# Gate weights loaded in an earlier stage, a place of its own for one raw tile, and other slots for two weight units in a fused mLSTM and mixture kernel

## The chip, the cores and the metric

The kernel runs on one core of one Trainium2 chip. The metric is the device time of the program in microseconds (us), median of several executions of the same program on the same inputs. Less is better.

## The reference

Three stages follow one another, all in fp32:

```python
x = mlstm(q, k, v, i_gate, f_gate, o_gate)        # (2, 8, 768, 40) -> x: 1536 tokens x 320
h = x @ w_in                                      # 320 x 2048
x = np.maximum(0.01 * h, h) @ w_out               # 2048 x 320
logits = x @ w_gate                               # 320 x 8
P = np.exp(logits - logits.max())
for _ in range(8):
    P /= P.sum(1, keepdims=True) + 1e-09
    P /= P.sum(0, keepdims=True) + 1e-09
    P *= 1536 / 8
out = sum(P[:, e:e+1] * (np.maximum(x @ w1[e], 0) @ w2[e]) for e in range(8))   # w1: 320 x 1024, w2: 1024 x 320
```

The last stage is dense: every token goes through all 8 experts, weighted by its column of P.

## The kernel before, in words

Precision first. Every product of two fp32 matrices is made of fp32r pieces: a factor is split into a high part (an ACT copy, `high7` L207 or L198) and a low part (the factor minus its high part, `low7` L210, `rest7` L214, L199, on DVE or POOL), and the product is the sum of three or four matmuls.

**First part** (up to the line `ctx.enter_context(tc.manual_schedule())`, L720). The attention runs in chunks of 128 tokens beside the first feed-forward, which goes through 96 steps of `up` (L520) and `down` (L532). Functions hang on these steps by number (`step(g, fn)`); in this part the framework may still reorder the instructions of each engine. The weights `w_in` and `w_out` come through three slots of the pool tag `raw`, loaded from the SP queue. Near the end of this part the first third of what the next stage needs is made: the tiles of x for the first half of the tokens (q = 0, class `Position`, x0), and the weights of expert units 0, 1 and 2.

**Second part.** From that line on the order written in the code is the order on each engine. The 8 experts make 32 units (`experts`, class `Products`, 256 hidden columns each; e0_3 is unit 3, e1_0 unit 4). The tokens are in two halves q, so there are 64 passes, in the order `order` (L818): units 0, 1, 2 with q = 0, then with q = 1, then unit 3 with both, unit 4 with both, and so on. The hidden layer of a pass, `up_c(i)` (L837), is a two by two block product done with seven block products instead of eight: seven calls of `product` (four matmuls each, L830 to L833) on sums and differences of blocks of the weights and of x. Four PSUM banks hold the results; ACT, DVE and POOL form from them the hidden tiles `hh` (high) and `hl` (low). `down_c(i)` (L880) multiplies these with `w2` for six token tiles (L157 to L159), in three PSUM banks by turns, and adds each result to `acc` (DVE L899 to L903, and ACT L897 for every second tile of unit 0).

The loop at the end emits `up_c(i+1)` and then `down_c(i)`. I call that **step i+1**: step 0 is `up_c(0)` alone, step 6 is `up_c(6)` with `down_c(5)`. Extra work hangs in by `when(g, slot, fn)` or `hook(g, slot, fn)`: slots 0 to 6 of g lie in `up_c(g+1)`, one behind each of its seven products, slots 7 to 12 in `down_c(g)`, one behind each tile. So (g, slot) always lies in step g+1. In this stretch hang:

- the x tiles of the second half of the tokens (x1). For each third p of them: `repeat` (POOL copies), `turn` (four transposes on TensorE into the one bank of `ps_s`, and an ACT copy into the raw tile, twice), `sums` (four subtractions, DVE), and the split into X[1] (`high` on ACT, `low` on DVE, `rest` on POOL). X[1] is first read by pass 3.
- the gate: the weights `wg` (loaded and split at L733 to L740), four `logits` in step 2, `logits_turn` and the maximum in step 3, and the eight rounds of row and column division in steps 4 to 7, two in each: `columns` on TensorE at slots 2 and 8, then `columns_end` and `rows` at slots 4 and 10, eight short DVE operations (L803 to L806, L793 to L796) that the next `columns` needs.
- the weights of units 3 and on: `load1` (ten DMAs into a `raw` slot), `sums` (four POOL operations, L186), `split1` in two halves (ACT copy L207, POOL L210 and L214), `load2`, `split2` (ACT L198, POOL L199).

The pool tag `raw` has three slots for all raw tiles of this stretch; a new tile takes over the slot of an earlier one and waits until that one's last use is over. Three lines show how the extra work is hung in:

```python
        when(g, s, x1[p].turn, k, ps_s)                    # L927
    for n in range(3, NU):
        u, g = experts[n], max(2 * n - 4, 3)               # L953: unit 3 has g = 3, unit 4 has g = 4
        hook(g - 2, 0, u.load1)
```

Of the kernel before, what the change touches and what calls it, by code (L numbers as in the profile page):

```python
# [37 lines left out]
def mlstm_moe_kernel(ctx, tc, qp, q3, kp, kn, vn, gates_in, og, cst_in, scr_in, w_in, w_out, w_gate, w1, w2, out):  # L38
# [35 lines left out]
    rc = cst[0:R, P + GV + 8:P + GV + 14]  # L74

# [140 lines left out]
    class Position:  # L216
# [62 lines left out]
    with ExitStack() as st1:  # L279
# [451 lines left out]

    wgr = cp.tile([P, 4, E], F32, tag="wgr", name="wgr")
    nc.gpsimd.memset(wgr, 0.0)  # L733
    for h in range(2):
        nc.sync.dma_start(wgr[:, 2 * h], w_gate[:, h])
        for r in (0, 2):
            nc.sync.dma_start(wgr[r * KM:(r + 1) * KM, 2 * h + 1], w_gate[h * KM:(h + 1) * KM, 2])
    wg = cp.tile([P, 4, 2, E], F32R, tag="wg", name="wg")
    nc.vector.tensor_copy(wg[:, :, 0, :], wgr)
    nc.vector.tensor_tensor(wg[:, :, 1, :], wgr, wg[:, :, 0, :].bitcast(F32), op=ALU.subtract)  # L740

    lT = cp.tile([2 * E, NT], F32, tag="lT", name="lT")
# [3 lines left out]
    K3 = 3 * KM  # L746

    def logits(q, i):
# [201 lines left out]
    when(-1, 3, experts[1].split2, GP)  # L950
    when(0, 12, experts[2].split2, GP)
    for n in range(3, NU):
        u, g = experts[n], max(2 * n - 4, 3)  # L953
        hook(g - 2, 0, u.load1)
        for k in range(4):
            hook(g, 8 + k, lambda u=u, k=k: u.sums(nc.gpsimd, (k,)))
        hook(g + 1, 8, lambda u=u: u.split1(0, nc.gpsimd, nc.gpsimd))
        hook(g + 1, 10, lambda u=u: u.split1(1, nc.gpsimd, nc.gpsimd))
        hook(g + 1, 12, u.load2)
        hook(g + 2, 8, lambda u=u: u.split2(nc.gpsimd))  # L960
# [117 lines left out]
```

## Time and profile before

| | before |
|---|---|
| median of 3 runs | 997.86 us (993.4 to 997.95) |
| the profiled execution: time, span | 997.24 us, 995.4 us |
| TensorE (PE) busy | 957.5 us, 96% of the span |
| VectorE (DVE), ScalarE (ACT), GpSimd (POOL) busy | 598.0, 485.7, 613.0 us |
| mean granted TensorE clock | 0.966 |

The span is the time from the first to the last instruction of the profiled execution. PE is the matrix engine, PEld its weight loads. The granted clock is a share of 2.4 GHz; TensorE has two levels, 1.0 (2.4 GHz) and 0.5 (1.2 GHz), so a stretch with 0.81 spent 0.38 of its time at 1.2 GHz. In rows of the timeline a value in brackets is the engine's idle time before the instruction and what ended it.

### The profile page before, as it was taken

The numbers are of one execution on the slowest core, as the hardware profiler recorded it, in microseconds if no ns is written. First come the engines' busy times: TensorE is split into PE (matmuls) and PEld (weight loads), VectorE is DVE, ScalarE is ACT, GpSimd is POOL, SyncE is SP. The second block draws the span as 40 slices with busy tenths as digits, with TensorE's granted clock in tenths as the row PEclk, the third lists the DMA queues.
The fourth block names the chain that finished last, engine by engine and source line by source line (L and its number), as shares of the span: only waits on it lengthen the run. The fifth ranks groups of instructions, "written<-read, shape, count | busy, mean of one in ns | idle before, by whom it ended". The sixth has DMA issues, their size and how long they took to land.

```text
span 995.4 us, 16898 instructions
## 1 busy us (share of the span) xinstructions
PE 957.5 (96%) x6188; PEld 924.0 (93%) x6188; DVE 598.0 (60%) x1159; ACT 485.7 (49%) x953; POOL 613.0 (62%) x616
## 2 busy tenths in 40 slices
PE   8699899999998997999999999999999999999998
PEld 4599898999997787899999999999999999999998
DVE  6989524142464566756656666666656566665655
ACT  4646344534655433564545454454545454454542
POOL 4553643443474434677777767677777767777762
PEclk9579999999997998999999999999999999999999
DMA  8544212011110200111111111111111111111102
GB/s 274 195 152 134 86 54 75 29 52 38 27 57 1 64 2 14 48 36 42 49 49 36 35 52 45 43 36 41 51 48 36 36 47 47 46 36 36 47 1 80
DMA packets 57160, 56.63 MB, mean 57 GB/s; under 512 B 7558, under 2 KB 47670, under 8 KB 57078
## 3 DMA queue, kind: packets, MB, share of 16 engines
q1 hardware_dynamic: 57078, 55.56, 18.6%
q8 instruction: 48, 0.79, 0.3%
q14 instruction: 34, 0.28, 0.1%
HBM read 53.57 MB, written 1.97 MB: 56 GB/s over the span
## 4 chain that ended last, share of the span: by engine, by line
PE 79%; DVE 9%; ACT 3%; POOL 3%; issue 2%; DMA 2%; SPq 1%; DVEq 0%; ACTq 0%; POOLq 0%
PE y L157 11%; PE y L158 11%; PE y L159 11%; PE b L833 8%; PE b L830 7%; PE b L832 7%; PE b L831 7%; PE ha L150 6%; PE ya L157 2%; PE ya L159 2%; PE ya L158 2%; PE yps L456 2%; PE sps L442 1%; PE zps L460 1%; DMA raw_a<-in_w_out_dram 1%
## 5 line engine op out<-in xcount | busy, mean ns | idle before, releaser
L852 POOL TENSOR_TENSOR hl<-c,hh 128x384 fp32r<-128x384 f32 x192 | 196.6, 1024 | 201.1 <-ACT c L851 176.5
L157 PE MATMUL y<-w_e,hh 128*128 128x320 f32 x768 | 238.7, 311 | 1.8 <-ACT acc L897 0.9
L158 PE MATMUL y<-w_e,hh 128*128 128x320 f32 x768 | 237.3, 309 | 0.0
L159 PE MATMUL y<-w_e,hl 128*128 128x320 f32 x768 | 236.8, 308 | 0.0
L903 DVE SCALAR_TENSOR_TENSOR acc<-y,Pg,acc 128x320 f32<-128x320 f32 x336 | 179.3, 548 | 63.7 <-PE y L159 56.1
L850 ACT ACTIVATE hh<-c 128x384 fp32r<-128x384 f32 x192 | 99.7, 519 | 226.9 <-DVE c L849 226.9
L830 PE MATMUL b<-X,w_e 128*128 128x384 f32 x448 | 154.5, 345 | 2.5 <-DVE s L861 2.0
L832 PE MATMUL b<-X,w_e 128*128 128x384 f32 x448 | 153.6, 343 | 2.2 <-POOL w_e L210 2.2
L833 PE MATMUL b<-X,w_e 96*128 96x384 f32 x448 | 154.1, 344 | 1.3 <-POOL w_e L214 1.3
L831 PE MATMUL b<-X,w_e 128*128 128x384 f32 x448 | 152.5, 340 | 0.0
L157 PEld LDWEIGHTS y<-w_e,hh 128*128 128x128 f32 x768 | 144.3, 188 | 3.9 <-DVE acc L899 1.5
L158 PEld LDWEIGHTS y<-w_e,hh 128*128 128x128 f32 x768 | 144.3, 188 | 0.0
L159 PEld LDWEIGHTS y<-w_e,hl 128*128 128x128 f32 x768 | 144.1, 188 | 0.0
L529 POOL TENSOR_TENSOR hla<-gg,hha 128x256 fp32r<-128x256 f32 x90 | 76.7, 856 | 85.5 <-ACT hha L528 72.5
L150 PE MATMUL ha<-xT,w_a 128*128 128x256 f32 x768 | 115.1, 293 | 6.8 <-DVE xT L269 3.5
L150 PEld LDWEIGHTS ha<-xT,w_a 128*128 128x128 f32 x768 | 105.1, 198 | 11.8 <-DVE xT L269 4.0
L851 ACT ACTIVATE c<-c 128x384 f32<-128x384 f32 x192 | 100.8, 525 | 17.4
L849 DVE TENSOR_TENSOR c<-b,s 128x384 f32<-128x384 f32 x192 | 100.5, 551 | 13.1 <-PE b L833 8.0
L868 DVE SCALAR_TENSOR_TENSOR hl<-b,hh 128x384 fp32r<-128x384 f32 x64 | 35.7, 558 | 103.1 <-ACT hh L867 103.1
L830 PEld LDWEIGHTS b<-X,w_e 128*128 128x128 f32 x448 | 86.0, 192 | 3.9 <-DVE s L861 2.9
L832 PEld LDWEIGHTS b<-X,w_e 128*128 128x128 f32 x448 | 85.6, 191 | 2.8 <-POOL w_e L210 2.8
L833 PEld LDWEIGHTS b<-X,w_e 96*128 96x128 f32 x448 | 85.8, 191 | 1.9 <-POOL w_e L214 1.9
(159 smaller groups left out, 1555.7 us busy)
## 6 DMA issues: line engine op xcount, KB each, us to landing
raw_e<-in_w_dram SPq DMA_DIRECT2D x32, 320.0 KB, 2.9
raw_e<-in_w_dram SPq DMA_DIRECT2D x62, 128.0 KB, 2.2
raw_e<-in_w_dram SPq DMA_DIRECT2D x248, 32.0 KB, 1.8
raw_a<-in_w_in_dram SPq DMA_DIRECT2D x8, 768.0 KB, 5.0
raw_a<-in_w_out_dram SPq DMA_DIRECT2D x8, 640.0 KB, 4.4
R<-in_kp_dram SPq DMA_DIRECT2D x11, 256.0 KB, 2.7
R<-in_qp_dram SPq DMA_DIRECT2D x11, 256.0 KB, 3.6
R<-in_vn_dram SPq DMA_DIRECT2D x11, 184.5 KB, 2.5
```

The lines of the kernel that those rows point to most:

```text
L150: nc.tensor.matmul(h_ps, t1[:, ws, c * P:(c + 1) * P], xt[:, xs, t0:t0 + n], start=(j == 0), stop=(j == len(MM1) - 1),)
L157: nc.tensor.matmul(y_ps, a, t2[:, c, :], start=first, stop=False)
L158: nc.tensor.matmul(y_ps, a, t2[:, 2 + c, :], start=False, stop=False)
L159: nc.tensor.matmul(y_ps, b, t2[:, c, :], start=False, stop=last)
L830: nc.tensor.matmul(bank, f[:, 0], b[:, 0], start=fresh, stop=False, skip_group_check=not fresh)
L831: nc.tensor.matmul(bank, f[:, 0], b[:, 2], start=False, stop=False, skip_group_check=not fresh)
L832: nc.tensor.matmul(bank, f[:, 2], b[:, 0], start=False, stop=False, skip_group_check=not fresh)
L833: nc.tensor.matmul(bank, f[0:K3, 1], b[0:K3, 1], start=False, stop=True, skip_group_check=not fresh)
L849: nc.vector.tensor_tensor(c, part, plus, op=ALU.add)
L851: nc.scalar.activation(c, c, AF.Relu)
L852: nc.gpsimd.tensor_tensor(hl[a][b], c, hh[a][b].bitcast(F32), op=ALU.subtract)
L903: nc.vector.scalar_tensor_tensor(out=o, in0=y, scalar=Pg[:, 2 * HP * q + t, e:e + 1], in1=o, op0=ALU.mult, op1=ALU.add)
```

## The change

1. The gate weights `wg` and their raw tile `wgr` move to a pool that lives through the whole kernel. Their six DMAs (`load_gate`, hung at step 64 of the first feed-forward) and their two DVE operations (`split_gate`, at step 70) are now in the first part. The clearing of `wgr` goes from POOL to DVE.
2. The raw tile of x for p = 1 (second half of the tokens) is a tile `rawE` of its own. The tile `lT` of the transposed logits, which had a place of its own, becomes a `raw` slot.
3. The x1 work hangs at other slots: the third p = 1 two slots earlier and its split later, the third p = 2 two slots earlier. `split2` of unit 1 moves from (-1, 3) to (-1, 6).
4. Unit 3: `sums` from (3, 8 to 11) to (2, 0 to 3), `split1` from (4, 8) and (4, 10) to (3, 0) and (3, 7), `load2` from (4, 12) to (3, 9), `split2` from (5, 8) to (4, 0). Unit 4: `load1` from (2, 0) to (2, 5), `sums` from (4, 8 to 11) to (4, 1 to 4), `split1` from (5, 8) and (5, 10) to (5, 0) and (5, 7), `load2` from (5, 12) to (5, 9), `split2` from (6, 8) to (6, 0). Units 5 and on stay.

```diff
+    wg = const.tile([P, 4, 2, E], F32R, tag="wg", name="wg")
+    wgr = const.tile([P, 4, E], F32, tag="wgr", name="wgr")
+    def load_gate():
+        nc.vector.memset(wgr, 0.0)
+        for h in range(2):
+            nc.sync.dma_start(wgr[:, 2 * h], w_gate[:, h])
+            for r in (0, 2):
+                nc.sync.dma_start(wgr[r * KM:(r + 1) * KM, 2 * h + 1], w_gate[h * KM:(h + 1) * KM, 2])
+    def split_gate():
+        nc.vector.tensor_copy(wg[:, :, 0, :], wgr)
+        nc.vector.tensor_tensor(wg[:, :, 1, :], wgr, wg[:, :, 0, :].bitcast(F32), op=ALU.subtract)
...
-        def turn(self, k, pool):
+        def turn(self, k, pool, home=None):
...
-                self.raw = wp.tile([P, 7, 2 * P], F32, tag="raw", name=f"rawx_{self.nm}", bufs=3)
+                self.raw = home or wp.tile([P, 7, 2 * P], F32, tag="raw", name=f"rawx_{self.nm}", bufs=3)
...
+        step(64, load_gate)
+        step(70, split_gate)
...
-    lT = cp.tile([2 * E, NT], F32, tag="lT", name="lT")
...
+        if 'lT' not in gate_state:
+            gate_state['lT'] = wp.tile([2 * E, NT], F32, tag="raw", name="lT", bufs=3)
+        lT = gate_state['lT']
...
+    rawE = cp.tile([P, 7, 2 * P], F32, tag="rawE", name="rawE")
     for p in (1, 2):
-        when(-1, (0, 5)[p - 1], x1[p].repeat, copy_rest)
-    for g, s, p, k in ((-1, 4, 1, 0), (-1, 6, 1, 1), (0, 2, 2, 0), (0, 5, 2, 1)):
-        when(g, s, x1[p].turn, k, ps_s)
-    for p, times in enumerate((((-1, 0), (-1, 1), (-1, 2), (-1, 3)), ((0, 3), (0, 4), (0, 6), (0, 7)), ((0, 10), (0, 11), (1, 0), (1, 1)))):
+        when(-1, (0, 2)[p - 1], x1[p].repeat, copy_rest)
+    for g, s, p, k in ((-1, 2, 1, 0), (-1, 4, 1, 1), (0, 0, 2, 0), (0, 3, 2, 1)):
+        when(g, s, x1[p].turn, k, ps_s, rawE if p == 1 else None)
+    for p, times in enumerate((((-1, 0), (-1, 1), (-1, 3), (-1, 4)), ((0, 1), (0, 2), (0, 4), (0, 5)), ((0, 8), (0, 9), (0, 11), (1, 0)))):
         for k in range(2):
             if p:
-                when(0, (0, 8)[p - 1] + k, x1[p].sums, V, k)
+                when(*((-1, 5), (-1, 6), (0, 6), (0, 7))[2 * p - 2 + k], x1[p].sums, V, k)
...
-    when(-1, 3, experts[1].split2, GP)
+    when(-1, 6, experts[1].split2, GP)
...
-        u, g = experts[n], max(2 * n - 4, 3)
-        hook(g - 2, 0, u.load1)
+        u, g = experts[n], 2 * n - 4
+        if n < 5:
+            times = ((1, 0), (2, 0), (3, 0), (3, 7), (3, 9), (4, 0)) if n == 3 else ((2, 5), (4, 1), (5, 0), (5, 7), (5, 9), (6, 0))
+        else:
+            times = ((g - 2, 0), (g, 8), (g + 1, 8), (g + 1, 10), (g + 1, 12), (g + 2, 8))
+        when(*times[0], u.load1)
...
```

Three places in the order of the instructions. (In the changed kernel L186 to L242 stand 15 lines lower in the file, L849 to L899 eight lines, so L210 is L225 there and L899 is L907.)

**POOL, steps 4 to 6, before.** `hl11_4` is the low part of a hidden tile of pass 4, `raw1_e0_3` the raw weights of unit 3, `w10_e0_3` and `w11_e0_3` their split halves. Pass 6 is the first that reads these halves; its own `hl` tiles are `hl11_6` and so on.

```order
L852 TENSOR_TENSOR hl01_4_3925<-c01_4_3984,hh01_4_3921 128x384
L186 TENSOR_TENSOR raw1_e0_3_3622<-raw1_e0_3_3622 128x256 x4
L852 TENSOR_TENSOR hl11_5_4063<-c11_5_4099,hh11_5_4059 128x384
L852 TENSOR_TENSOR hl10_5_4062<-c10_5_4122,hh10_5_4058 128x384
L852 TENSOR_TENSOR hl01_5_4061<-c01_5_4131,hh01_5_4057 128x384
L210 TENSOR_TENSOR w10_e0_3_4154<-raw1_e0_3_3622,w10_e0_3_4154 128x4x128
L214 TENSOR_TENSOR w10_e0_3_4154<-raw1_e0_3_3622,w10_e0_3_4154 32x4x128
L186 TENSOR_TENSOR raw1_e1_0_3797<-raw1_e1_0_3797 128x256 x2
L210 TENSOR_TENSOR w11_e0_3_4155<-raw1_e0_3_3622,w11_e0_3_4155 128x3x128
L214 TENSOR_TENSOR w11_e0_3_4155<-raw1_e0_3_3622,w11_e0_3_4155 32x3x128
```

**POOL, steps 4 and 5, after the change.**

```order
L225 TENSOR_TENSOR w10_e0_3_3940<-raw1_e0_3_3623,w10_e0_3_3940 128x4x128
L229 TENSOR_TENSOR w10_e0_3_3940<-raw1_e0_3_3623,w10_e0_3_3940 32x4x128
L860 TENSOR_TENSOR hl11_4_3931<-c11_4_3961,hh11_4_3927 128x384
L860 TENSOR_TENSOR hl10_4_3930<-c10_4_3984,hh10_4_3926 128x384
L860 TENSOR_TENSOR hl01_4_3929<-c01_4_3993,hh01_4_3925 128x384
L225 TENSOR_TENSOR w11_e0_3_3941<-raw1_e0_3_3623,w11_e0_3_3941 128x3x128
L229 TENSOR_TENSOR w11_e0_3_3941<-raw1_e0_3_3623,w11_e0_3_3941 32x3x128
L214 TENSOR_TENSOR w2_e0_3_4082<-raw2_e0_3_4028,w2_e0_3_4082 128x640
L201 TENSOR_TENSOR raw1_e1_0_3842<-raw1_e1_0_3842 128x256 x2
L860 TENSOR_TENSOR hl11_5_4073<-c11_5_4114,hh11_5_4069 128x384
```

Unit 3's split, which stood behind `hl01_5`, now stands around the `hl` tiles of pass 4, and two of unit 4's sums stand before `hl11_5`.

**DVE, end of step 1, before.** `s2_1` and `c..` are the sums that `up_c(1)` makes from PSUM, `rawx_1_1` and `rawx_1_2` the raw x of the thirds p = 1 and 2, X1 the split x, `acc0<-y0_0` the eviction of the first tile of `down_c(0)`.

```order
L868 SCALAR_TENSOR_TENSOR hl00_1_3465<-b0_1_3457,hh00_1_3461 128x384
L849 TENSOR_TENSOR c10_1_3519<-b2_1_3459,s1_1_3470 128x384
L849 TENSOR_TENSOR c01_1_3534<-b3_1_3460,s1_1_3470 128x384
L210 TENSOR_TENSOR X1_3365<-rawx_1_1_3423,X1_3365 128x4x128
L899 COPY acc0_3364<-y0_0_3541 128x320
L210 TENSOR_TENSOR X1_3365<-rawx_1_1_3423,X1_3365 128x3x128
L242 TENSOR_TENSOR rawx_1_2_3491<-rawx_1_2_3491 128x256 x2
L899 COPY acc0_3364<-y0_2_3561 128x320
```

**DVE, the same stretch, after the change.**

```order
L876 SCALAR_TENSOR_TENSOR hl00_1_3468<-b0_1_3460,hh00_1_3464 128x384
L225 TENSOR_TENSOR X1_3364<-rawE_3365,X1_3364 128x4x128
L857 TENSOR_TENSOR c10_1_3526<-b2_1_3462,s1_1_3473 128x384
L225 TENSOR_TENSOR X1_3364<-rawE_3365,X1_3364 128x3x128
L857 TENSOR_TENSOR c01_1_3537<-b3_1_3463,s1_1_3473 128x384
L257 TENSOR_TENSOR rawx_1_2_3480<-rawx_1_2_3480 128x256 x2
L907 COPY acc0_3363<-y0_0_3544 128x320
L257 TENSOR_TENSOR rawx_1_2_3480<-rawx_1_2_3480 128x256 x2
L907 COPY acc0_3363<-y0_2_3563 128x320
```

Before the eviction of `y0_0` there are now both low parts of p = 1 and two sums of p = 2, where one low part stood.

**ACT, steps 0 and 1, after the change.** `px0_1_2` is the bank with the first transposes of the third p = 2, `s0_1` the first copy that `up_c(1)` needs, `w2_e0_1` unit 1's second weights (before, `w2_e0_1` stood ahead of `hh00_0`).

```order
L875 ACTIVATE hh00_0_3370<-b0_0_3366 128x384
L251 ACTIVATE rawE_3365<-px1_1_1_3427 128x4x128
L858 ACTIVATE hh10_0_3372<-c10_0_3439 128x384
L859 ACTIVATE c10_0_3439<-c10_0_3439 128x384
L858 ACTIVATE hh01_0_3371<-c01_0_3450 128x384
L859 ACTIVATE c01_0_3450<-c01_0_3450 128x384
L213 ACTIVATE w2_e0_1_3457<-raw2_e0_1_3310 128x640
L863 ACTIVATE s0_1_3472<-b0_1_3460 128x384
L251 ACTIVATE rawx_1_2_3480<-px0_1_2_3481 128x4x128
L222 ACTIVATE X1_3364<-rawE_3365 128x4x2x128
L222 ACTIVATE X1_3364<-rawE_3365 128x3x2x128
L858 ACTIVATE hh11_1_3467<-c11_1_3503 128x384
```

The copy of `px0_1_2` stands behind `w2_e0_1` and `s0_1`, and the split of p = 1 right behind it, ahead of pass 1's first hidden tile.

## Rows read from the trace of the kernel before

**Rows 1.** The profile page: busy time of the engines; the chain that ended last.

```profile
PE 957.5 (96%) x6188; PEld 924.0 (93%) x6188; DVE 598.0 (60%) x1159; ACT 485.7 (49%) x953; POOL 613.0 (62%) x616
...
PE 79%; DVE 9%; ACT 3%; POOL 3%; issue 2%; DMA 2%; SPq 1%; DVEq 0%; ACTq 0%; POOLq 0%
```

**Rows 2.** Windows, steps 0 to 8: stretch, length, busy (count) of PE, PEld, DVE, ACT, POOL, PEclk.

```profile
300.76:312.57 11.81, 7.63 (x39) 6.78 (x37) 4.42 (x10) 6.24 (x12) 5.60 (x8) 0.76 0.02 2
312.57:327.86 15.29, 14.03 (x75) 13.12 (x73) 10.46 (x17) 9.95 (x19) 7.82 (x10) 0.85 0.00 1
327.86:344.70 16.84, 16.17 (x97) 13.01 (x96) 9.18 (x16) 6.80 (x14) 7.93 (x7) 1.00 0.33 94
344.70:357.10 12.40, 12.11 (x81) 11.25 (x81) 6.44 (x18) 4.76 (x10) 3.06 (x3) 1.00 0.01 2
357.10:369.97 12.87, 11.33 (x70) 10.67 (x69) 9.48 (x28) 4.56 (x10) 4.13 (x5) 1.00 0.00 0
369.97:382.05 12.08, 11.07 (x71) 10.68 (x69) 8.41 (x24) 5.81 (x11) 5.25 (x7) 1.00 0.01 1
382.05:400.50 18.45, 14.31 (x71) 12.62 (x69) 11.32 (x29) 5.58 (x11) 10.40 (x12) 0.81 0.07 20
400.50:415.23 14.73, 12.87 (x71) 12.01 (x69) 11.99 (x29) 5.40 (x11) 9.12 (x9) 0.88 0.21 58
415.23:425.52 10.29, 10.29 (x67) 10.20 (x66) 7.33 (x14) 8.02 (x16) 7.45 (x9) 1.00 0.12 34
```

**Rows 3.** Waits of PE from 300 to 425 us: total, times, longest.

```profile
PE cps L800 <- DVE Pg L796: 4.5, 4, 1.7
PE px L235 <- ACT rawx L236: 2.3, 1, 2.3
PE b L832 <- POOL w_e L210: 2.2, 2, 1.8
PE b L830 <- DVE s L861: 2.0, 2, 1.9
```

**Rows 4.** Timeline of step 0: start, length, instruction, idle time before it.

```profile
304.25 0.60 PE L235 MATMUL px<-cst,x 128*128 128x128 f32 x4
305.13 0.18 DVE L739 CAST wg<-wgr 128x32 fp32r<-128x32 f32 x1 [7.54 <-DMA wgr<-in_w_gate_dram]
...
310.13 0.99 POOL L214 TENSOR_TENSOR X<-rawx,X 32x384 fp32r<-32x384 f32 x1
...
311.15 0.60 ACT L236 ACTIVATE rawx<-px 128x512 f32<-128x512 f32 x1 [1.24 <-POOL X L214]
```

**Rows 5.** Groups of instructions from 300 to 425 us: busy us, mean ns.

```profile
L851 ACT ACTIVATE c<-c 128x384 f32<-128x384 f32 x27 | 14.2, 525 | 2.2
...
L207 ACT ACTIVATE X<-rawx 128x1024 fp32r<-128x1024 f32 (+1 forms) x6 | 5.6, 946 | 2.4 <-DVE rawx L242 2.4
```

**Rows 6.** Timeline of ACT and POOL around the start of step 6.

```profile
380.50 1.78 ACT L207 ACTIVATE w_e<-raw_e 128x1024 fp32r<-128x1024 f32 x2
...
381.64 1.28 POOL L210 TENSOR_TENSOR w_e<-raw_e,w_e 128x512 fp32r<-128x512 f32 x1
...
386.90 0.99 POOL L214 TENSOR_TENSOR w_e<-raw_e,w_e 32x384 fp32r<-32x384 f32 x1
```

**Rows 7.** Timeline of DVE and POOL: the same operation alone, and beside POOL.

```profile
395.06 0.26 DVE L806 SCALAR_TENSOR_TENSOR Pg<-Pg,cs 128x96 f32<-128x96 f32 x1
...
400.45 1.34 DVE L806 SCALAR_TENSOR_TENSOR Pg<-Pg,cs 128x96 f32<-128x96 f32 x1
...
400.11 1.57 POOL L199 TENSOR_TENSOR w_e<-raw_e,w_e 128x640 fp32r<-128x640 f32 x1
```

**Rows 8.** Timeline of the SP queue and of DVE in the first feed-forward.

```profile
41.30 0.35 SPq L417 DMA_DIRECT2D R<-in_kn_dram  x1
45.56 0.33 SPq L99 DMA_DIRECT2D raw_a<-in_w_in_dram  x1
...
94.97 0.57 DVE L128 TENSOR_SCALAR raw_a<-raw_a 128x768 int32<-128x768 int32 x1 [0.41 <-DMA raw_a<-in_w_in_dram]
```

More of the change, by code (lines that the diff above doesn't have):

```diff
@@ L730, in mlstm_moe_kernel @@
     Pg = cp.tile([P, NCK, E], F32, tag="Pg", name="Pg")
[L732 to L740, printed above, removed]
-    lT = cp.tile([2 * E, NT], F32, tag="lT", name="lT")
     rs = cp.tile([P, NCK], F32, tag="rs", name="rs")
@@ L746, in mlstm_moe_kernel @@
     K3 = 3 * KM
+    gate_state = {}
     def logits(q, i):
@@ L755, in logits @@
                              start=(n == 0), stop=(n == len(terms) - 1))
+        if 'lT' not in gate_state:
+            gate_state['lT'] = wp.tile([2 * E, NT], F32, tag="raw", name="lT", bufs=3)
+        lT = gate_state['lT']
         nc.scalar.activation(lT[:, (2 * q + i) * NQ:(2 * q + i + 1) * NQ], lps[0:2 * E, 0:NQ], AF.Copy)
-    gate_state = {}
     def logits_turn():
         ltp = gate_state['ltp'] = ps_s.tile([P, NCK, 2, E], F32, tag="b1", name="ltp")
+        lT = gate_state['lT']
         for t in range(NCK):
@@ L948, in mlstm_moe_kernel @@
             when(7 + q, (0, 0, 1, 1, 2, 2)[t], scale_first, q, t)
-    when(-1, 3, experts[1].split2, GP)
+    when(-1, 6, experts[1].split2, GP)
     when(0, 12, experts[2].split2, GP)
     for n in range(3, NU):
-        u, g = experts[n], max(2 * n - 4, 3)
-        hook(g - 2, 0, u.load1)
-        for k in range(4):
[L956 to L960, printed above, removed]
+        u, g = experts[n], 2 * n - 4
[4 more added lines that the diff above has]
+        when(*times[0], u.load1)
+        for k in range(4):
+            when(times[1][0], times[1][1] + k, u.sums, GP, (k,))
+        when(*times[2], u.split1, 0, GP, GP)
+        when(*times[3], u.split1, 1, GP, GP)
+        when(*times[4], u.load2)
+        when(*times[5], u.split2, GP)
     up_c(0)
```

## Prediction

> **What bounds the kernel now.** I read the page first: TensorE is busy for 96% of the span and holds 79% of the chain that ended last [rows 1]. So time is saved only where TensorE waits or runs at the low clock. Then I cut the part that the change touches into steps [rows 2]. Step 8 takes 10.29 us with TensorE busy throughout, and so do the steps after it. Steps 0 to 7 take 114.5 us; there TensorE idles, and four of them show a granted clock under 1. From a clock c the time at 1.2 GHz is 2 × (1 − c) × length: 5.7 us in step 0, 4.6 in step 1, 7.0 in step 6, 3.5 in step 7. Such a stretch costs about half its length where TensorE has work. The waits of TensorE from 300 to 425 us name the causes [rows 3]: the rounds of the gate (4.5 us in four waits), one wait for the copy of transposed x (2.3), POOL's split of a weight (2.2 at L832, more at L833) and one bank that DVE was late to read (2.0, of which 1.9 in one wait). Outside this part the change touches only the first feed-forward.
>
> **The first feed-forward.** Six small DMAs and two DVE operations are added. In the new order the first two DMAs stand on the SP queue behind the load of `kn` at 41.3 us, where SP waits until 45.56 for a slot anyway [rows 8]; the others stand in similar waits, and an issue takes 0.33 to 0.35 us by the rows around them. The two DVE operations take about 0.2 each (0.18 for the cast [rows 4]) and come before 94.97 us, where DVE waits 0.41 us for a weight DMA [rows 8], which is their cover. Without it they would cost 0.4. I take 0, with ends −0.2 and +0.5: a shift of this early order can move a wait either way.
>
> **Steps 0 to 2, term A.** In step 0 DVE stood 7.54 us before the cast of the gate weights [rows 4], and the sums of `up_c(0)` were queued behind it; that made the 1.9 us wait for a bank. The second transposes of p = 1 waited 2.3 us because the ACT copy before them needed a raw slot that POOL's `rest` held until 311.12 [rows 4]. Both go: the gate weights are ready, and `rawE` needs no slot. A product takes 0.70 us (five from 300.76 to 304.25), a set of transposes 0.60 [rows 2, 4]. So `up_c(0)` needs 7 × 0.70 + 2 × 0.60 = 6.1 us and ends at 306.9 instead of 312.6, which is **5.7 us** earlier.
>
> What is late next? ACT and DVE. I laid the new order out by hand with these durations. After 306.9 ACT has four activations for pass 0, `w2_e0_1` and `s0_1` ahead of the copy of `px0_1_2`. At about 0.53 each [rows 5] that is 3.2 us. Between them ACT waits some 2.5 us for DVE, because two sums of `rawE` stand ahead of `c01_0`, and each has to let a `rest` of POOL end (0.99 for the shorter [rows 4]). How DVE fares beside POOL is seen from one operation: 0.26 us alone, 1.34 beside POOL's 1.57 us `split2`, in which it ended just after POOL did [rows 7]. So the copy ends near 313.2; TensorE, which is through four products and one set of transposes at 311.2 (0.3 and 0.7 of it lost to banks), waits 2.0 us.
>
> Behind that copy ACT does both splits of p = 1 (0.95 each [rows 5]), three more activations and `hh00_1`, until 317. Then DVE must do `hl00_1`, two low parts, `c10`, `c01` and two sums before it evicts `y0_0`, near 322.6. TensorE needs that for its fourth tile, since there are three banks. It could be there at 318.6 at the full clock; if the clock falls at the 2.0 us wait, as it did in step 0, at 320.7. Either way the fourth tile begins near 322.6, and `down_c(0)` ends, with three more tiles of 0.9 ((10.29 − 7 × 0.70) / 6 [rows 2]) and a short wait, at 325.7 instead of 327.86. Of the 5.7 us I keep **2.2**.
>
> Step 2 has 16.17 us of work in 16.84 [rows 2]. Its waits were for the sums and copies that were late in step 1, and in the new order these are done: **+0.7**. The slot for `lT` is that of unit 2's second weights, free before the first logits are copied: 0. A = **2.9**. The bounds: 6.4 if nothing takes the place of the removed waits; −0.5 if the two new waits bring one more stretch at 1.2 GHz like that of step 7 (1.75) and DVE is 1.7 later still. I take 2.9 because DVE's blocked operations are the nearest row there is.
>
> **Steps 3 to 7, term B.** In step 6 pass 6 began at 382.05, but POOL split unit 3's weights from 381.64 to 387.89 [rows 6]. That gave the waits at L832 and L833 and the 7.0 us at the low clock. In the new order unit 3 is split around the `hl` tiles of pass 4, some 10 us before it is read. Its raw weights take over unit 1's slot, which is free before step 2, so the load is in time. Step 7 lost 1.7 us in one wait for the gate's rows [rows 3] and then 3.5 us at the low clock; its DVE chain ran beside unit 4's split [rows 7], which now comes one step earlier. Steps 4 to 7 have the same gate work, so I take the undisturbed step 5 as the model for steps 6 and 7: 18.45 − 12.08 + 14.73 − 12.08 = **+9.0**.
>
> What the moved work costs where it goes: in step 4 ACT copies `w11_e0_3` before it evicts the second tile. Two copies of 1024 and 768 elements take 1.78 us [rows 6], so this one 3/7 of it, **−0.75**, and TensorE waits for that eviction. Below it is 0, if a bank is free. In step 5 two sums of unit 4 and a late `hl11_5` lie beside the first gate chain. A blocked operation waits for the end of POOL's current one; laid out, three operations come 0.2, 0.2 and 0.15 us late: **−0.55**. The ends are 0 and 4 × 1.08 = 4.3 (all four long operations like that of rows 7). The other chains keep the neighbours that they had, or have some slack. The sums in step 3 run before the gate's chain there. B = 9.0 − 1.3 = **7.7**.
>
> Sum: 2.9 + 7.7 = 10.6. The profiled execution took 997.24 us, 0.6 under the median of the runs shown, so **986.6 us**. About 0.5% (5 us) is what a measurement of this kernel can tell from no change.
>
> **The rivals.**
> - *ACT and DVE keep up.* A is 6.4: 997.24 − 14.1 = 983.1. For it: TensorE waited little in step 1 so far (14.03 busy of 15.29 [rows 2]). Against it: the new DVE order puts more ahead of the first eviction, and ACT's 16.2 us of work in steps 0 and 1 must fit a shorter stretch.
> - *New waits eat all of A.* A is −0.5: 990.0. For it: two waits of about 2 us close together, and waits of 1.7 and 1.9 us came with a low clock before.
> - *POOL's moved work blocks the gate's chains.* This one ends slower. The eight chains of steps 4 to 7 have four long DVE operations each. Where POOL runs sums and splits behind each other, a chain gets as late as in step 7: a wait of 1.7 us [rows 3] and 3.5 us at half speed, together 3.4 us. Three such chains undo the gain, five bring 986.6 + 17 = 1003.6. It decides when POOL has an instruction of a microsecond or more under every long operation. Against it: in the new order only the late chain of steps 4 and 6, which have a product or two of slack, and the early one of step 5 have POOL work beside them. The Trainium skill (SBUF — State Buffer, section "Who interferes with whom") says that a DVE instruction with two SBUF inputs and a GpSimd instruction that reads SBUF exclude each other for the whole instruction; by it alone, with every chain hit, this rival would be the forecast. The trace agrees as to the single operation (0.26 against 1.34).
> - *Unit 3 is still late*, if its load or a slot for its split holds it up: B is gone, but not its costs, and 995.6 us results. Against it: the slots are free several us earlier.
>
> **How the numbers follow.** Forecast 0.60; ACT and DVE keep up 0.16; A eaten 0.15; chains blocked 0.04; unit 3 late 0.05. The range from 982 to 994.5 takes in the first three with the bounds of the small terms, and one more low-clock stretch or two (1.75 each); outside are the last two rivals and the tails. Faster by over 0.5% (under 992.9): nearly all of the first two and most of the third, 0.85. Within 0.5%: 0.11. Slower: 0.04.
>
> **What would show it.** Right: no wait for `wgr` on DVE in the second part; `up_c(0)` in 6 to 6.5 us; a wait of 1.5 to 2.5 us before the second transposes of p = 2 and another before the fourth tile of `down_c(0)`; steps 0 to 2 shorter by 2 to 4 us in sum; no wait for POOL at L832 and L833 of pass 6; steps 6 and 7 each near 12.1 us at clock 1.00; step 4 longer by 0.7. Wrong would be: a low clock in steps 4 to 7, a wait of TensorE for `Pg` over 1.5 us, or a longer first feed-forward.

## The result, and the profile after

Median of 4 runs 985.4 us (984.06 to 986.44) against 996.51 us (993.4 to 997.95, 4 runs): ratio 0.989, interval 0.9864 to 0.9915. The forecast was 986.6. The profiled execution took 986.44 us, its span is 984.5 us (995.4 before), its mean granted clock 0.974.

The page of the changed kernel, busy times (compare [rows 1]):

```profile
PE 949.2 (96%) x6188; PEld 919.7 (93%) x6188; DVE 595.6 (60%) x1160; ACT 485.7 (49%) x953; POOL 614.4 (62%) x615
```

Windows of the changed kernel, steps 0 to 7, columns as in [rows 2]:

```profile
300.59:306.38 5.79, 5.79 (x38) 5.72 (x37) 2.40 (x5) 4.97 (x10) 2.06 (x6) 1.00 0.00 1
306.38:324.57 18.19, 13.61 (x74) 12.41 (x73) 14.71 (x25) 11.74 (x22) 12.96 (x12) 0.91 0.11 30
324.57:340.03 15.46, 15.46 (x96) 13.16 (x95) 7.75 (x13) 6.19 (x13) 8.89 (x9) 1.00 0.12 34
340.03:352.41 12.38, 12.07 (x81) 11.22 (x80) 6.42 (x17) 4.77 (x10) 3.79 (x4) 1.00 0.10 28
352.41:365.99 13.58, 11.31 (x71) 10.65 (x69) 10.21 (x28) 6.24 (x12) 7.43 (x7) 1.00 0.00 0
365.99:379.01 13.02, 11.05 (x71) 10.66 (x69) 9.17 (x24) 4.98 (x10) 7.65 (x9) 1.00 0.24 68
379.01:391.11 12.10, 11.05 (x71) 10.66 (x69) 9.35 (x29) 5.60 (x10) 6.02 (x6) 1.00 0.00 1
391.11:404.26 13.15, 11.50 (x70) 10.49 (x69) 10.41 (x29) 4.54 (x9) 6.65 (x7) 1.00 0.23 65
```

The last three columns are the granted clock, the DMA share and GB/s. Set beside [rows 2], the stretch ahead of step 0 is as long as it was (300.76 and 300.59 us), and steps 0 to 7 shrank from 114.47 to 103.67 us. These 10.8 us are the whole difference of the spans (10.9); step 8 takes 10.24 us (10.29). Steps 0 to 2 gave 4.5 us (43.94 to 39.44), steps 3 to 7 gave 6.3 (70.53 to 64.23). Only step 1 still shows a low clock: 2 × 0.09 × 18.19 = 3.3 us at 1.2 GHz, where four steps had such stretches before.

Waits of PE from 300 to 415 us in the changed kernel (total, times, longest; compare [rows 3]):

```profile
PE cps L808 <- DVE Pg L804: 5.7, 5, 2.0
PE px L250 <- ACT rawx L251: 1.6, 1, 1.6
PE y L172 <- DVE acc L907: 1.6, 2, 1.3
PE b L838 <- DVE c L857: 1.4, 1, 1.4
PE y L172 <- ACT acc L905: 1.3, 1, 1.3
```

POOL's split of a weight has left the list, and so has the sum that DVE made too late. In their place stand the copy of `rawx` for the third p = 2, a `c` sum, an eviction on DVE and one on ACT (step 4), and the gate's wait has grown from 4.5 to 5.7 us.

Timeline of DVE, POOL, ACT and PE in step 1 of the changed kernel (rows chosen, in order of time):

```profile
307.01 2.63 POOL L229 TENSOR_TENSOR X<-rawx,X 32x512 fp32r<-32x512 f32 x2
...
307.74 2.18 DVE L257 TENSOR_TENSOR rawE<-rawE 128x256 f32<-128x256 f32 x2
...
309.85 0.55 DVE L857 TENSOR_TENSOR c<-b,s 128x384 f32<-128x384 f32 x1
...
310.44 0.45 PE L838 MATMUL b<-X,w_e 128*128 128x384 f32 x1 [1.36 <-DVE c L857]
...
312.41 0.59 ACT L251 ACTIVATE rawx<-px 128x512 f32<-128x512 f32 x1
...
313.05 1.12 PE L250 MATMUL px<-cst,rr 128*128 128x128 f32 x4 [1.62 <-ACT rawx L251]
...
321.28 0.41 PE L172 MATMUL y<-w_e,hh 128*128 128x320 f32 x1 [1.32 <-DVE acc L907]
```

Two sums of `rawE` (2.18 us for the pair) lie beside two `rest` of POOL (2.63). `c01` of pass 0 stands behind them on DVE and is done at 310.40; TensorE waits 1.36 us for its bank. ACT copies `px` only after that pass's activations, so the second transposes of p = 2 begin at 313.05 (forecast near 313.2). The fourth tile begins at 321.28 (322.6), `down_c(0)` ends at 324.57 (325.7). The fourth tile follows the eviction of the first on DVE:

```profile
320.74 0.48 DVE L907 COPY acc<-y 128x320 f32<-128x320 f32 x1
```

### The profile page after: what moved, and what is told of

Its sections match the earlier page's. It is cut to its first block, busy times and chain, and to the rows that moved or that the text cites. A ratio compares the mean times of both kernels' runs of the same rounds, so it can differ in the third digit from the quotient of the medians.

```text
span 984.5 us, 16900 instructions
## 1 busy us (share of the span) xinstructions
PE 949.2 (96%) x6188; PEld 919.7 (93%) x6188; DVE 595.6 (60%) x1160; ACT 485.7 (49%) x953; POOL 614.4 (62%) x615
## 3 DMA queue, kind: packets, MB, share of 16 engines
HBM read 53.57 MB, written 1.97 MB: 56 GB/s over the span
## 4 chain that ended last, share of the span: by engine, by line
PE 84%; DVE 7%; ACT 4%; DMA 2%; issue 1%; POOL 1%; SPq 1%; ACTq 0%; DVEq 0%; POOLq 0%
PE y L172 11%; PE y L173 11%; PE y L174 11%; PE b L841 8%; PE b L838 8%; PE b L839 8%; PE b L840 7%; PE ha L165 7%; PE ya L172 3%; PE ya L174 2%; PE ya L173 2%; PE yps L471 2%; PE sps L457 1%; PE zps L475 1%; DVE c L857 1%
## 5 line engine op out<-in xcount | busy, mean ns | idle before, releaser
L838 PE MATMUL b<-X,w_e 128*128 128x384 f32 x448 | 152.9, 341 | 1.4 <-DVE c L857 1.4
L839 PE MATMUL b<-X,w_e 128*128 128x384 f32 x448 | 151.6, 338 | 0.0
L841 PE MATMUL b<-X,w_e 96*128 96x384 f32 x448 | 151.6, 338 | 0.0
L840 PE MATMUL b<-X,w_e 128*128 128x384 f32 x448 | 151.1, 337 | 0.0
L201 POOL TENSOR_TENSOR raw_e<-raw_e 128x256 f32<-128x256 f32 x116 | 84.6, 739 | 4.5
```

The lines of the kernel that those rows point to most:

```text
L838: nc.tensor.matmul(bank, f[:, 0], b[:, 0], start=fresh, stop=False, skip_group_check=not fresh)
L839: nc.tensor.matmul(bank, f[:, 0], b[:, 2], start=False, stop=False, skip_group_check=not fresh)
L840: nc.tensor.matmul(bank, f[:, 2], b[:, 0], start=False, stop=False, skip_group_check=not fresh)
L841: nc.tensor.matmul(bank, f[0:K3, 1], b[0:K3, 1], start=False, stop=True, skip_group_check=not fresh)
```

## The experiments

Three comparisons, each with its own runs of the kernel before: medians 996.71 us (22 runs) for the first four kernels, 995.92 (13) for the next four, 995.11 (11) for the last four.

**One part alone: the units.** The kernel before with the new slots of units 3 and 4 and nothing else:

```diff
-        u, g = experts[n], max(2 * n - 4, 3)
...
+        u, g = experts[n], 2 * n - 4
+        if n < 5:
+            times = ((1, 0), (2, 0), (3, 0), (3, 7), (3, 9), (4, 0)) if n == 3 else ((2, 5), (4, 1), (5, 0), (5, 7), (5, 9), (6, 0))
...
```

> The kernel before with the new slots of units 3 and 4 alone. If the parts add up as the prediction has it: steps 4 to 7 take 51.9 us as in the changed kernel (58.1 before), steps 0 to 2 stay at 43.9, and the time falls by about 6.2 us to 990.3. Rival 1, the parts are tied together (the units can be split early only because lT and rawE change the raw slots): a new wait for a raw slot or a load, and less than 3 us gained. Rival 2, the low clock of step 6 came from the disturbed steps before it and not from the late split: nearly all of the 11 us.

Median 990.75 us, ratio 0.9934 (0.9909 to 0.9959). Window of step 7:

```profile
394.18:407.30 13.12, 11.53 (x70) 10.52 (x69) 10.38 (x29) 4.53 (x9) 6.60 (x7) 1.00 0.25 66
```

Steps 3 to 7 take 64.19 us, as in the changed kernel (64.23), step 6 of them 12.10 at clock 1.00; steps 0 to 2 stay (43.64). So the gain that the prediction calls term B, its surprise in step 7 included, comes from the units' slots alone.

**The changed kernel without the units.** The two rules of the diff above changed back.

> The changed kernel with the old slots of units 3 and 4. If the parts add up: steps 0 to 2 take 39.4 us as in the changed kernel, steps 4 to 7 stay near 58.1, and the time falls by about 4.5 us to 992. Rival, the late split is partly an effect of the gate and x work: steps 6 and 7 fall by more than 2 us without being touched.

Median 993.1 us, ratio 0.997 (0.995 to 0.9989). Windows, steps 1 and 6:

```profile
306.50:324.68 18.18, 14.80 (x74) 13.60 (x73) 14.71 (x25) 11.74 (x22) 12.96 (x12) 0.81 0.11 30
...
377.44:395.91 18.47, 14.18 (x71) 12.50 (x69) 11.34 (x29) 5.60 (x11) 10.44 (x12) 0.82 0.07 19
```

Steps 0 to 2 take 39.43 us and steps 3 to 7 70.48, step 7 of them 14.71 at a clock of 0.88. The two terms add: 4.5 and 6.3.

Step 1 has the same instructions as in the changed kernel and the same two first waits (1.35 and 1.62 us), but TensorE spent 2 × 0.19 × 18.18 = 6.9 us of it at 1.2 GHz instead of 3.3. It is no longer for it: 18.18 against 18.19 us. The wait of 1.32 us before the fourth tile has all but gone, and that tile begins 14.88 us after the start of the step, 14.90 in the changed kernel. DVE's eviction sets this time, and the low clock used up a wait.

**The gate weights alone.** The kernel before, with the first part of the change only (`wg` and `wgr` in the lasting pool, two more steps of the first feed-forward):

```diff
...
+        step(64, load_gate)
+        step(70, split_gate)
...
```

> The kernel before with the gate weights in the first feed-forward and nothing else. By the prediction's reasoning the 1.9 us wait in step 0 goes, POOL's rest of p = 0 is done some 3 us earlier, and a wait of about 2.4 us for the raw slot stays: up_c(0) takes 9 to 9.5 us (11.8 before), the time falls by 2.5 to 3.5 us to 993.5. Rival: what is gained in step 0 is given back in step 1, where ACT and DVE are late in any case: less than 1 us. Other rival: the wait for the slot goes with it, and 5 us or more are gained. In the first feed-forward all theories expect no change over 0.5 us.

Median 994.17 us, ratio 0.9972 (0.9953 to 0.9991). Windows of steps 0 and 7, then the first of the waits of PE in steps 0 to 2:

```profile
299.73:309.34 9.61, 6.53 (x38) 5.86 (x37) 4.97 (x8) 6.24 (x12) 5.53 (x7) 0.95 0.00 1
...
396.84:411.56 14.72, 11.51 (x70) 10.49 (x69) 11.97 (x29) 5.40 (x11) 9.15 (x9) 1.00 0.21 58
```

```profile
PE px L250 <- ACT rawx L251: 3.0, 1, 3.0
```

Step 0 is 2.2 us shorter. The wait for the copy into the raw slot stays: POOL's `rest` still ends last before that copy. The wait is 3.0 us instead of 2.3, but the gate weights are not the reason: in the kernel with the units alone, whose step 0 was left as it was, it is 3.0 as well, with less time at the low clock (granted clock 0.88 instead of 0.76) and the same length of step 0 (11.83 and 11.81 us). Steps 0 to 2 gain 2.6 us (41.34).

Step 7 has the instructions of the kernel before, took 14.72 us at a clock of 1.00, and 14.73 before at 0.88. At the full clock TensorE waits for `Pg` twice (1.76 and 1.45 us), at the lower one once (1.75).

**All but the gate weights.** The changed kernel with `wg` and `wgr` loaded and split where they were before:

```diff
...
-        step(64, load_gate)
-        step(70, split_gate)
...
```

> The changed kernel with the gate weights loaded in the second part as before (rawE, the new slots of x and of the units stay). If the cast on DVE is what held step 0: DVE idles until about 305 us, step 0 takes 2 us more, and since ACT and DVE are behind each other through step 1 most of it stays: steps 0 to 2 take 41 to 42 us and the time is 987 to 988. Rival: step 1 waits for ACT anyway, so the cast costs nothing: 985.4. Other rival: without the gate weights the clock falls in step 0 as before and all of the gain of steps 0 to 2 is lost: 990.

Median 989.9 us, ratio 0.9931 (0.9902 to 0.996). Window of step 0:

```profile
302.44:309.97 7.53, 6.06 (x39) 5.74 (x37) 2.56 (x6) 4.08 (x8) 1.64 (x6) 1.00 0.03 2
```

Steps 0 to 2 take 42.81 us, more than the 41 to 42 of the theory, and the total is over its 987 to 988: DVE stands 7.59 us before the cast, its work comes later, and TensorE has a new wait of 2.9 us for an eviction in step 1. So `rawE` and the new slots of x without the gate weights are worth 1.1 us, the gate weights without them 2.6, and both 4.5. Each hides the other's wait; neither alone frees step 0.

**The copy of px earlier.** The changed kernel; one sum of `rawE` goes behind `c01` of pass 0, and `split2` of unit 1 (POOL) to a later slot:

```diff
-                when(*((-1, 5), (-1, 6), (0, 6), (0, 7))[2 * p - 2 + k], x1[p].sums, V, k)
+                when(*((-1, 6), (-1, 6), (0, 6), (0, 7))[2 * p - 2 + k], x1[p].sums, V, k)
...
-    when(-1, 6, experts[1].split2, GP)
+    when(0, 10, experts[1].split2, GP)
```

> The changed kernel with two queue orders of steps 0 and 1 altered: the first two sums of rawE stand behind c01 of pass 0 on DVE, and split2 of unit 1 (ACT copy and POOL) goes from the end of step 0 to the end of step 1. If the waits of 1.4 and 1.6 us in step 1 are what the prediction says (c01 behind two sums that wait for POOL, the copy of the transposes behind w2 on ACT): both shrink to under 0.5 us, the clock does not fall there, step 1 takes 15.5 to 16.5 us (18.2 in the changed kernel), the time is 2 us less, 983.3. Rival: step 1 is bound by the eviction of the first tile on DVE alone, which waits for hh00 and what is behind it: the early waits go but the late one grows by as much, and step 1 stays at 18 us.

Median 987.1 us, ratio 0.9908 (0.9881 to 0.9934). Window of step 1:

```profile
308.22:325.94 17.72, 14.89 (x74) 13.71 (x74) 15.30 (x25) 11.47 (x22) 11.13 (x10) 0.81 0.00 1
```

A miss: 15.5 to 16.5 us were expected. The waits shrank (1.36 and 1.62 us became 1.03 and 1.25, the fourth tile's 1.32 became 0.26), the clock was low for longer, 2 × 0.19 × 17.72 = 6.7 us instead of 3.3, and step 1 is only 0.47 us shorter. The longer low clock is not what kept it: step 1 without the new units had 6.9 us of it and lost nothing. The fourth tile again follows DVE's eviction of the first and begins 14.42 us after the start of the step, 0.48 earlier than in the changed kernel, which is the whole gain. So the rival has the better of it: the new orders bring that eviction forward by half a microsecond and no more, and it is argued, not shown, that at the full clock the rest would have become a longer wait there.

**The first eviction earlier.** The changed kernel; the two sums of p = 2 behind the first evictions, its split later:

```diff
-...((0, 8), (0, 9), (0, 11), (1, 0))
+...((0, 9), (0, 11), (0, 12), (1, 1))
...
-                when(*((-1, 5), (-1, 6), (0, 6), (0, 7))[2 * p - 2 + k], x1[p].sums, V, k)
+                when(*((-1, 5), (-1, 6), (0, 7), (0, 9))[2 * p - 2 + k], x1[p].sums, V, k)
```

> The changed kernel with the sums of x third p = 2 hung behind the first and third tile of down_c(0) instead of ahead of it, and its split one or two slots later. If the sums ahead of the eviction are the cause of the 1.3 us wait before the fourth tile: it goes to under 0.5 us, step 1 takes about 17 us (18.2), step 2 stays at 15.5, the time is 1.2 us less, 984.2. Rival: the split of p = 2 now comes too late for the logits of step 2, which read X[1]: step 2 grows by 1 us or more and the sum of steps 0 to 2 stays at 39.4.

Median 985.9 us, ratio 0.991 (0.9885 to 0.9934). Windows, steps 1 and 2:

```profile
304.79:321.93 17.14, 13.55 (x73) 12.37 (x73) 13.68 (x22) 11.00 (x21) 12.01 (x11) 0.90 0.11 32
321.93:338.38 16.45, 16.23 (x96) 13.00 (x95) 9.47 (x16) 6.80 (x14) 9.69 (x10) 1.00 0.11 32
```

Step 1 gives 1.05 us and step 2 takes 0.99 back. The rival's number came out (39.38 us for steps 0 to 2), its cause only in part. Some 1.7 us of DVE's work moved into step 2 (7.75 to 9.47 us busy). There TensorE stops before two products whose bank is read late (0.18 us is the one wait that the list of waits shows, for DVE), and for about 0.2 us before the second logits.

**POOL's work at other places.** The changed kernel; unit 3's second split a slot later, two of unit 4's sums and its last splits into other steps:

```diff
-... ((1, 0), (2, 0), (3, 0), (3, 7), (3, 9), (4, 0)) if n == 3 else ((2, 5), (4, 1), (5, 0), (5, 7), (5, 9), (6, 0))
+... ((1, 0), (2, 0), (3, 0), (3, 8), (3, 9), (4, 0)) if n == 3 else ((2, 5), (4, 1), (5, 0), (6, 0), (5, 9), (6, 8))
...
-            when(times[1][0], times[1][1] + k, u.sums, GP, (k,))
+            when(times[1][0], 9 + k if n == 4 and k > 1 else times[1][1] + k, u.sums, GP, (k,))
```

> The changed kernel with three pieces of the units' work at other places: the second half of unit 3's split one slot later (behind the eviction of the second tile on ACT), two of unit 4's sums behind the hl tiles of pass 5 instead of beside the gate's chain, the second half of unit 4's split in up_c(7) and its split2 in down_c(6). If ACT's copy ahead of the eviction costs 0.7 in step 4, POOL beside the gate's chain 0.9 in step 5 and 1.0 in step 7: step 4 goes from 13.6 to 12.9, step 5 from 13.0 to 12.3, step 7 from 13.2 to 12.2, the time falls by 2.3 us to 983. Rival: the gate's chains are late because of DVE's own evictions and not because of POOL: only step 4 changes, 984.7.

Median 981.9 us, ratio 0.9863 (0.9833 to 0.9893). Windows, steps 4 to 7:

```profile
350.15:363.01 12.86, 11.31 (x71) 10.66 (x69) 9.51 (x27) 6.24 (x12) 6.67 (x7) 1.00 0.00 0
363.01:375.08 12.07, 11.05 (x71) 10.66 (x69) 8.99 (x25) 4.98 (x10) 7.39 (x8) 1.00 0.26 73
375.08:387.66 12.58, 11.13 (x71) 10.57 (x70) 9.83 (x29) 4.86 (x9) 6.73 (x7) 1.00 0.00 1
387.66:399.75 12.09, 11.05 (x71) 10.66 (x70) 9.34 (x29) 5.27 (x10) 5.43 (x6) 1.00 0.17 44
```

Steps 4, 5 and 7 lose their excess (0.72, 0.95 and 1.06 us), step 6 pays 0.48, since the two moved sums lie beside the late chain of step 5 (L814 0.51 and L802 0.40 us there; L812 took 0.54, beside `hl` tiles) and the sums of `up_c(6)` queue behind it: 61.97 us instead of 64.23. POOL does the same instructions in both; their neighbours on DVE and ACT differ, and with the splits ACT's copies of the same weights moved too.

**All three together.** The last three edits in one kernel.

> All three together. If the waits are independent: steps 0 to 2 take 36 to 37 us (39.4), steps 3 to 7 62 us (64.2), the time is 5 to 5.5 us under the changed kernel, 980. Rival: ACT bounds steps 0 and 1 whatever the order (it has 16 us of work there): steps 0 to 2 stay over 38 us and the time is 982.5.

Median 985.13 us, ratio 0.9898 (0.9868 to 0.9927). A miss: steps 0 to 2 take 38.52 us instead of 36 to 37, over the 38 of the rival. The waits that are left in them name DVE (1.2 and 0.8 us) and ACT (1.0), so ACT alone is not shown to bound them. Steps 0 to 8 take 110.8 us (113.91 in the changed kernel, 111.64 with POOL's places alone).

**POOL reading, beside the chain.** The kernel with POOL's places, and three POOL additions on a scratch tile beside the first gate chain of steps 6 and 7:

```diff
+    dummy = cp.tile([P, 2, NQ], F32, tag="dummy", name="dummy")
+    when(3, 0, nc.gpsimd.memset, dummy, 0.0)
...
+    def beside():
+        for _ in range(3):
+            nc.gpsimd.tensor_tensor(dummy[:, 0], dummy[:, 0], dummy[:, 1], op=ALU.add)
+    when(5, 3, beside)
+    when(6, 3, beside)
```

> The kernel e7 with three additional POOL additions of 128x384 on a scratch tile (they read and write SBUF) behind the first hl tile in steps 6 and 7, so that they lie beside the first gate chain of each. If a chain operation waits for the end of POOL's current instruction: the chain of eight DVE operations goes from 2.04 us to 3.2 to 3.6, the wait for Pg at slot 8 from about 1.0 (1.45 in step 6) to 2.2 to 2.9, steps 6 and 7 take 1.2 us more each, up to 2.9 more where the clock falls too. Rival, the chain's late operations in step 5 and 7 of the changed kernel had another cause (DVE's own queue): no change, steps of 12.6 and 12.1.

One execution, 991.11 us. Timeline of POOL, DVE and PE around the first chain of step 6:

```profile
383.99 3.15 POOL L981 TENSOR_TENSOR dummy<-dummy 128x384 f32<-128x384 f32 x3
...
384.05 0.97 DVE L812 TENSOR_SCALAR cs<-cs 128x8 f32<-128x8 f32 x1
...
385.29 0.89 DVE L814 SCALAR_TENSOR_TENSOR Pg<-Pg,cs 128x96 f32<-128x96 f32 x1
...
386.50 0.67 DVE L802 TENSOR_SCALAR rs<-rs 128x12 f32<-128x12 f32 x1
...
387.87 0.71 PE L808 MATMUL cps<-Pg,ones 128*128 128x96 f32 x2 [3.37 <-DVE Pg L804]
```

The chain takes 3.96 us instead of 2.04 in the kernel without the additions, more than the 3.2 to 3.6 expected; the wait for it is 3.37 us (2.2 to 2.9 expected), and step 6 takes 15.65 us at a clock of 0.89 instead of 12.58 at 1.00 (step 7: 15.55, 0.89, instead of 12.09). The first clearing of the scratch tile lies in step 4, which takes 13.51 us instead of 12.86; that is a side effect of the experiment.

**POOL only writing.** The same, with a clearing of 128x768 in place of each addition:

```diff
-            nc.gpsimd.tensor_tensor(dummy[:, 0], dummy[:, 0], dummy[:, 1], op=ALU.add)
+            nc.gpsimd.memset(dummy, 0.0)
```

> The same as e9 with three clearings of 128x768 instead of the additions: POOL writes SBUF and reads nothing, some 0.9 us each. If any POOL instruction holds the chain: as e9. If only the reading side is shared for operations with two SBUF inputs: the two operations with two tensors from SBUF (Pg with cs, Pg with rs) keep their 0.26 us, and at most the two with a constant (128x8 and 128x12) are late; the wait grows by under 0.8 us.

One execution, 991.08 us. Timeline of the same stretch:

```profile
386.90 2.33 POOL L981 MEMSET dummy<- 128x768 f32 x3
386.97 0.69 DVE L812 TENSOR_SCALAR cs<-cs 128x8 f32<-128x8 f32 x1
...
387.93 0.26 DVE L814 SCALAR_TENSOR_TENSOR Pg<-Pg,cs 128x96 f32<-128x96 f32 x1
...
388.51 0.74 DVE L802 TENSOR_SCALAR rs<-rs 128x12 f32<-128x12 f32 x1
...
...
389.95 0.43 PE L808 MATMUL cps<-Pg,ones 128*128 128x96 f32 x2 [2.53 <-DVE Pg L804]
```

The two operations with a constant (L812, L802, which add 1e-09) are held up here too, the two with two tensors (L814, and L804 with 0.26 us) are not. The wait is 2.53 us, 1.1 more than without the clearings and more than the 0.8 expected; the two held operations are 0.52 and 0.57 us longer, which is all of it.

**The two candidates again.** First all three edits, then POOL's places alone, in one comparison.

> The kernel of e8 once more, to set it against e7 on one chip. Its steps 0 to 8 were 0.85 us shorter in the trace, its median 3.2 us longer. If that was the first part of the program, which differs from execution to execution: steps 0 to 8 again near 110.8 us and the median at or under that of e7, near 982. Rival: its order costs something outside steps 0 to 8: again 2 us or more behind e7.

> The kernel of e7 once more beside e11: steps 0 to 8 near 111.7 us, median 982 to 983.5. If e7's 981.9 was a lucky draw of the first part, it comes out within 1 us of e11.

984.05 us (ratio 0.9894, 0.9871 to 0.9917; 6 runs) and 985.85 us (0.9897, 0.9877 to 0.9917; 5 runs). Steps 0 to 8 repeat to 0.1 us (110.76 and 111.71), the total does not. Windows of the first 60 us and of step 0 in two executions of the same kernel (POOL's places), the first from its first comparison, the second from this one:

```profile
0.00:60.00 60.00, 43.56 (x248) 31.60 (x248) 52.48 (x84) 32.41 (x55) 34.10 (x26) 0.80 0.67 221
...
298.37:304.16 5.79, 5.79 (x39) 5.72 (x38) 2.41 (x5) 4.97 (x10) 2.06 (x6) 1.00 0.00 1
```

```profile
0.00:60.00 60.00, 45.79 (x232) 34.06 (x233) 51.67 (x84) 33.48 (x57) 34.12 (x25) 0.72 0.65 214
...
300.78:306.57 5.79, 5.79 (x39) 5.72 (x37) 2.41 (x5) 4.97 (x10) 2.05 (x6) 1.00 0.01 1
```

Step 0 began 2.4 us later in the second, after a first part with a lower clock. The total carries this scatter, so by the total neither candidate is shown faster than the changed kernel, which ran in another comparison; by steps 0 to 8 they are 2.2 and 3.1 us shorter.

## Why the prediction was right, and where its terms were not

The sign, the places and the sum were right: 10.8 us gained in steps 0 to 7 against a sum of 10.6. That the sum is right to 0.2 us is luck: two terms were off by 1.6 and 1.4 us and cancelled.

- **First feed-forward, 0.** Not contradicted, and not shown: step 0 began at 300.59 us instead of 300.76, but in the ten traces of kernels with this same first part it began anywhere from 297.37 to 302.89. Against that neither 0 nor the ends of −0.2 and +0.5 can be told apart, and it is chance that the two spans differ by just what steps 0 to 7 gained.
- **Term A, 2.9 forecast, 4.5 measured.** The way was the one laid out: no wait for `wgr`, a wait before the second transposes of p = 2 and one before the fourth tile. The sizes were too dear. `up_c(0)` took 5.79 us, not 6.1: a set of transposes takes 0.60 us, but the product behind it begins after 0.35. Up to the copy of the transposes the layout by hand was good (313.0 us, 313.2 said); behind it `hh00_1` ended at 316.50 instead of 317, and from there DVE needed 4.7 us to the end of the eviction instead of 5.6. So the fourth tile came 1.3 us earlier than said and `down_c(0)` ended 1.1 us earlier. Step 2 gained 1.4 us instead of 0.7: before, TensorE stopped three times in it, and a stop costs more than its idle time, since the first matmul behind it was counted busy for 0.44 or 0.45 us instead of 0.34 and the end of the last one before it, which otherwise overlaps the next, stands alone. So the 16.17 us were not all work; now the step takes 15.46.
- **Term B, 7.7 forecast, 6.3 measured.** Step 6 is the copy of step 5 as said (12.10, clock 1.00), and step 4 paid 0.71 us for the ACT copy (0.75 said). Step 5 paid 0.94 (0.55 said): L812 took 0.75 us instead of 0.17 and L814 0.62 instead of 0.26 beside the two sums, and the wait for `Pg` reached 1.97 us, over the 1.5 that was to be a mark against the forecast. The clock stayed at 1.00 all the same. The long operations of that chain in the changed kernel:

```profile
372.19 0.75 DVE L812 TENSOR_SCALAR cs<-cs 128x8 f32<-128x8 f32 x1
...
373.21 0.62 DVE L814 SCALAR_TENSOR_TENSOR Pg<-Pg,cs 128x96 f32<-128x96 f32 x1
```

- **The price of the low clock** did not hold in three steps. The prediction counts half of a stretch at 1.2 GHz as lost, and a late gate chain as a wait of 1.7 us and 3.5 us at half speed, 3.4 in all. But traces with the same instructions in a step and a different clock show equal lengths: step 0 11.81 us with 5.7 us at 1.2 GHz (before) and 11.83 with 2.8 (units alone), step 1 18.19 with 3.3 and 18.18 with 6.9, step 7 14.73 with 3.5 and 14.72 with none. In steps 1 and 7 TensorE at the full clock waits for DVE instead, and in step 0 for the copy by ACT. The whole late step 7 cost 2.65 us over the undisturbed step 5. The terms A and B are mostly differences of lengths read from the rows and do not rest on this price; the lower end of A, the price of the third rival and the width of the range do. Step 6 had a clock of 0.81 or 0.82 in every trace with the late split, so what the low clock costs there is not shown.
- **The step that failed** is the model for step 7: "its DVE chain ran beside unit 4's split [rows 7], which now comes one step earlier", priced at nothing. It took 13.15 us, not 12.08.

Timeline of POOL and DVE around the end of step 6 and, for PE, of step 7 in the changed kernel:

```profile
390.24 0.55 DVE L812 TENSOR_SCALAR cs<-cs 128x8 f32<-128x8 f32 x1
...
390.72 1.02 POOL L225 TENSOR_TENSOR w_e<-raw_e,w_e 128x384 fp32r<-128x384 f32 x1
...
391.06 0.79 DVE L814 SCALAR_TENSOR_TENSOR Pg<-Pg,cs 128x96 f32<-128x96 f32 x1
...
391.82 1.02 POOL L229 TENSOR_TENSOR w_e<-raw_e,w_e 32x384 fp32r<-32x384 f32 x1
...
392.18 0.69 DVE L802 TENSOR_SCALAR rs<-rs 128x12 f32<-128x12 f32 x1
...
393.34 0.88 DVE L909 TENSOR_TENSOR acc<-y,acc 128x320 f32<-128x320 f32 x2
...
400.28 0.43 PE L808 MATMUL cps<-Pg,ones 128*128 128x96 f32 x2 [1.45 <-DVE Pg L804]
```

The same operation of that chain in the kernel with POOL's places:

```profile
387.60 0.26 DVE L814 SCALAR_TENSOR_TENSOR Pg<-Pg,cs 128x96 f32<-128x96 f32 x1
```

The split did not leave the gate's chains: it moved from the chain of step 7 to the late chain of step 6, where two operations beside it are 0.53 and 0.52 us longer (0.26 and 0.17 alone). A third, L812, is 0.38 us longer, but it lies beside the `hl` tiles that stand ahead of the split, and it is as long (0.54) with POOL's places. That chain itself had slack, as the prediction said (TensorE waits 0.20 us at its end), but the evictions and the sums of `up_c(7)` queue behind it on DVE. The products of step 7 end 5.97 us after its start, 5.31 in the kernel with POOL's places, and its wait for `Pg` is 1.45 instead of 1.04 us: 0.66 + 0.41 = 1.07, the whole excess. With POOL's places step 7 takes 12.09. That kernel moved ACT's copies together with POOL's part of the split; that POOL's work alone lengthens these DVE operations and the steps is shown by the run with added POOL additions.

Of the rivals, "ACT and DVE keep up" fell (three waits of 1.3 to 1.6 us in step 1, 4.5 instead of 6.4), "A eaten" fell, "unit 3 late" fell, and "POOL blocks the chains" was true of two chains in a mild form that cost 2.0 us. A dearer form of it is shown only with the added POOL work: steps of 15.6 us at a clock of 0.89.

## What to carry to other kernels

Cut a transition into steps, lay the order of each queue out by hand, and follow the engine that is late next: the sum here was right within 0.2 us by luck, its terms only within 1.6. Before a low clock gets a price, ask which engine ends the step: where DVE or ACT does, the slow matmuls may only fill a wait. When work moves from one place to another on a helper engine, price it at the neighbour that it gets and also at everything queued behind that neighbour; slack of the neighbour alone is no cover. And a cure that lacks its other half may show a quarter or a half of its worth (1.1 and 2.6 us alone, 4.5 together), so try both before dropping either.

## What the runs showed of the hardware

Beside the added POOL additions on SBUF tiles, short DVE operations of 0.17 to 0.26 us took 0.67 to 0.97; beside the POOL clearings, those with a constant took 0.69 and 0.74 and those with two SBUF tensors their usual 0.26. The reciprocals (0.20 and 0.23) and reductions (0.25) were not longer in either run. The Trainium skill (SBUF — State Buffer, "Who interferes with whom") has it that a DVE instruction with two SBUF inputs contends with a POOL instruction that reads SBUF and not with one that only writes it; the two runs agree (0.89 us beside the additions, 0.26 beside the clearings). The same section says that a DVE instruction in a mode that uses both ports contends with POOL. The operations with a constant, late in both runs, fit this, but that they were in such a mode no run here shows.

The time at the low clock did not follow the length of a wait: in step 1 waits of 1.36 and 1.62 us came with 3.3 us at 1.2 GHz, waits of 1.35 and 1.62 us on the same instructions with 6.9, shorter ones of 1.03 and 1.25 us with 6.7, and the single wait of 1.97 us in step 5 with none. What decides it is left open. Nor did a step get longer by it where DVE or ACT ended the step (18.19 and 18.18 us in step 1, 14.73 and 14.72 in step 7).
